# A kernel's opening rearranged: all of x ahead of the weights, and a first chunk of eight plain block products

## The chip, the cores and the metric

One core of one Trainium2 chip runs the whole program. The metric is the device time of one execution in microseconds (us). The kernel before takes 1982.69 us, the median of three runs (1981.05 to 1983.4). Every run is named fast, slow or unknown by its time and clock.

## The reference

```python
def reference(x, moe_w_in, moe_w_out):          # x (8, 3008, 256) f32; weights f64
    X = np.fft.fft(np.fft.fft(x, axis=1), axis=2).real.astype(np.float32)
    h = X.reshape(24064, 256) @ moe_w_in          # 256 x 2048
    g = h * np.clip(h + 3.0, 0.0, 6.0) / 6.0      # hardswish
    return (g @ moe_w_out).astype(np.float32)     # 2048 x 256
```

## The kernel before

The Fourier transform along the sequence (3008 = 47 x 64) is done in two stages of matrix products, for two batches (a pair) at a time; the one along the model dimension is folded into w_in. The MLP then goes over the tokens in chunks of eight steps. The steady state is full of TensorE work, and the change leaves it alone. What it touches is the opening.

Some filler products keep TensorE awake until the first data are there. Then eight blocks of x go through stage 1. Seven of them use `fold_first` and `stage1_first`; the last block (number 7) needs the longer `fold`. The products of stage 1 use 94 rows and 96 columns of the 128 x 128 array (`PR` = 94, `PZ` = 96).

```python
def stage1_first(pr, c, i):
    ...
    for k, (f, m, c0) in enumerate([(F[0:PR, 0:PZ], a[:, :, 0:P + 1], 0), (F[0:PR, 0:PZ], b, 1),
                                    (F[0:PR, 0:PZ], a[:, :, 1:P], P + 1), (FN[0:PR], b, P + 1)]):
        nc.tensor.matmul(ps[0:PZ, :, c0:c0 + m.shape[2]], f, m, start=(k == 0), stop=(k > 0),
                         skip_group_check=True)
    evict_z(pr, c, i, ps)      # ACT copies into a tile z; the queue SP writes it to DRAM
    ...
def keep_awake(n):
    ps = ps_h.tile([P, 2 * TB], F32, tag="uv", name="awake")
    for i in range(n):
        nc.tensor.matmul(ps[:], ones[:], Z[:], start=True, stop=True)
...
keep_awake(6)
```

The f64 weights come in 16 pieces, and each is converted by four engines: ACT takes the exponents out of the raw bits (`exponent_a`), TensorE joins them (`exponent_b`, called ex below), ACT shifts them back (`exponent_c`), VectorE takes the mantissa and multiplies (`mantissa`, `join`). Every second piece of w_in is followed by a fold of eight products of 0.43 us, whose last row travels through DRAM into the tile WN. Before the change, one piece lies behind each block of stage 1 and eight more follow:

```python
for c in range(NXC):
    if c + 2 < NXC:
        load_x(first, c + 2)
    load_w(c + 2)
    ...                               # fold_first, or fold for the last block
    on_scalar(c)                      # exponent_c of the piece before, exponent_a of this one
    on_vector(c)                      # mantissa, join
    for i in range(XC // 2):
        (stage1_first if c < NXC - 1 else stage1)(first, c, i)
    on_tensor(c)                      # exponent_b, and a fold after every second w_in piece
    ...
load_g(first, 0)                      # reads the results back for stage 2
for j in range(NXC, 15):              # seven more pieces (the sixteenth ahead of the first chunk)
    ...
```

A step of the MLP is `mlp1` (products u and v, made two steps ahead, then VectorE, two relus on ACT, two gates on VectorE), `combine` (sums on GpSimd) and `mlp2`: seven products in place of eight, in the manner of Strassen, for which w_out needs four combinations (`mix_w_out`, on VectorE).

## Time and profile before

| | before |
|---|---|
| median of 3 runs | 1982.69 us |
| span of the profiled run | 1978.3 us |
| TensorE busy | 1949.1 us, 99% of the span |
| first product of stage 1, last one | 10.5 us, 53.7 us |
| ninth set of seven products, the first behind the first chunk | 134.96 us |

The page names engines PE (TensorE matmul), PEld (its weight loads), DVE (VectorE), ACT (ScalarE), POOL (GpSimd) and SP (SyncE). L204 means line 204. In the chain of waits each line is a start, a duration, an engine and what it did; the chain is the work that ended last, followed backwards. In a timeline, the bracket at the end is how long the engine stood idle before, and what ended that. In the windows, PEclk is the granted TensorE clock as a share of full speed. The lines of before are shown in the prediction.

### The profile page before, as it was taken

Reading aid. Unit: us, or ns where it says so; the run is one execution under the profiler, and the core shown is the slowest. Engines: PE = TensorE matmul, PEld = TensorE weight load, DVE = VectorE, ACT = ScalarE, POOL = GpSimd, SP = SyncE. Lnnn points to the kernel's source line nnn. Section 1 sums busy time; section 2 is a strip of 40 time slices with the busy share of each in tenths; the row PEclk is TensorE's granted clock in tenths of the full one; section 3 lists DMA queues with packets and bytes.
Section 4 is the critical chain, followed back from the end, with each engine's and each line's share of the span. In section 5 each row is a group of like instructions: output and inputs, shape, how many; then the busy total and the mean of one; then the engine's idle time right before and its main releaser. Section 6 shows DMA issues by size and latency. Waiting matters only on the chain.

```text
span 1978.3 us, 27746 instructions
## 1 busy us (share of the span) xinstructions
PE 1949.1 (99%) x9178; PEld 1685.4 (85%) x9178; DVE 1433.5 (72%) x2775; ACT 687.9 (35%) x1164; POOL 1414.2 (71%) x1604
## 2 busy tenths in 40 slices
PE   8899999999999999999999999999999999999998
PEld 5588888888998888888898888888889888888887
DVE  5677767776787776776777776777678777777776
ACT  6533333333333333333333333333333333333332
POOL 4277778786687787777768877778667667666765
PEclk9999999999999999999999999999999999999999
DMA  9502211111111111221111221212110101111000
GB/s 307 136 26 61 51 41 46 49 49 35 27 36 51 41 49 48 54 59 24 36 32 30 63 55 44 56 41 54 37 22 23 30 14 25 26 24 28 17 20 20
DMA packets 149701, 93.31 MB, mean 47 GB/s; under 512 B 121739, under 2 KB 135055, under 8 KB 149558
## 3 DMA queue, kind: packets, MB, share of 16 engines
q1 hardware_dynamic: 139294, 57.86, 12.2%
q0 software_dynamic: 9472, 33.49, 5.9%
q8 instruction: 72, 1.18, 0.2%
q14 instruction: 71, 0.58, 0.1%
q10 hardware_dynamic: 792, 0.20, 0.0%
HBM read 54.19 MB, written 37.33 MB: 46 GB/s over the span
## 4 chain that ended last, share of the span: by engine, by line
PE 93%; DVE 2%; ACT 1%; issue 0%; DMA 0%; SPq 0%; DVEq 0%; ACTq 0%
PE acc L403 56%; PE v L334 16%; PE u L334 16%; PE ps L284 2%; PE ps L227 2%; DVE a L379 1%; DVE s L339 1%; ACT t L376 0%; ACT PM L509 0%; DVE o L461 0%; PE wps L574 0%; DVE u L360 0%; PE ps L224 0%; PE ex L514 0%; PE awake L597 0%
## 5 line engine op out<-in xcount | busy, mean ns | idle before, releaser
L393 POOL TENSOR_TENSOR c<-a 128x512 f32<-128x512 f32 (+1 forms) x383 | 478.2, 1248 | 431.4 <-PE acc L403 369.3
L403 PE MATMUL acc<-c,G 128*128 128x256 f32 (+1 forms) x3072 | 712.0, 375 | 0.0
L376 ACT ACTIVATE t<-u,half 128x512 f32<-128x512 f32 (+1 forms) x384 | 261.0, 680 | 1100.5 <-DVE u L349 1018.7
L403 PEld LDWEIGHTS acc<-c,G 128*128 128x128 f32 x3072 | 577.5, 190 | 72.7
L339 DVE SCALAR_TENSOR_TENSOR s<-qn,WN,u 128x256 f32<-128x256 f32 (+1 forms) x768 | 330.0, 471 | 354.3 <-PE u L334 354.0
L403 PE MATMUL acc<-a,G 128*128 128x256 f32 (+1 forms) x2304 | 551.2, 375 | 0.0
L403 PEld LDWEIGHTS acc<-a,G 128*128 128x128 f32 x2304 | 433.8, 190 | 55.9
L334 PE MATMUL v<-q,W 127*128 127x256 f32 (+1 forms) x1536 | 390.1, 376 | 4.4 <-DVE a L379 4.4
L334 PE MATMUL u<-q,W 128*128 128x256 f32 (+1 forms) x1536 | 388.3, 375 | 2.4 <-DVE a L379 2.1
L379 DVE SCALAR_TENSOR_TENSOR a<-t,u 128x512 f32<-128x512 f32 (+2 forms) x448 | 263.7, 600 | 104.9 <-ACT t L376 102.1
L334 PEld LDWEIGHTS u<-q,W 128*128 128x128 f32 x1536 | 285.7, 190 | 58.2 <-issue 14.8
L334 PEld LDWEIGHTS v<-q,W 127*128 127x128 f32 x1536 | 288.7, 190 | 45.1 <-DVE a L379 4.1
L393 POOL TENSOR_TENSOR c<-c,a 128x256 f32<-128x256 f32 (+1 forms) x383 | 274.8, 717 | 30.0
L393 POOL TENSOR_TENSOR c<-a,c 128x256 f32<-128x256 f32 (+1 forms) x383 | 274.6, 717 | 30.1
L349 DVE TENSOR_TENSOR u<-s,v 128x512 f32<-128x512 f32 x352 | 245.0, 696 | 37.7 <-PE v L334 0.8
L379 DVE SCALAR_TENSOR_TENSOR a<-t,v 128x512 f32<-128x512 f32 (+1 forms) x480 | 263.2, 564 | 0.0
L376 ACT ACTIVATE t<-v,half 128x512 f32<-128x512 f32 (+1 forms) x384 | 260.5, 678 | 0.0
L351 DVE TENSOR_TENSOR v<-v,s 128x512 f32<-128x512 f32 x352 | 243.7, 692 | 0.0
L393 POOL TENSOR_TENSOR r<-w,e 128x256 f32<-128x256 f32 (+1 forms) x94 | 90.8, 987 | 3.7
L411 ACT ACTIVATE e<-acc 128x512 f32<-128x512 f32 (+2 forms) x190 | 86.3, 545 | 3.4 <-PE acc L403 3.3
L461 DVE STREAM_TRANSPOSE o<-r 128x256 f32<-128x256 f32 (+1 forms) x192 | 72.5, 414 | 0.2
L239 ACT COPY z<-ps 96x512 f32<-96x512 f32 x64 | 37.2, 582 | 83.7 <-PE ps L227 65.2
(91 smaller groups left out, 780.2 us busy)
## 6 DMA issues: line engine op xcount, KB each, us to landing
out_dram<-o SPq DMA_DIRECT2D x746, 32.0 KB
zd<-z SPq DMA_DIRECT2D x32, 384.0 KB
g<-zd SPq DMA_DIRECT2D x48, 256.0 KB
xt<-in_x_dram POOLq DMA_DIRECT2D x21, 384.0 KB, 4.1
qn<-qd SPq DMA_DIRECT2D x19, 256.0 KB
st<-in_moe_w_in_dram POOLq DMA_DIRECT2D x8, 512.0 KB, 9.1
st<-in_moe_w_out_dram POOLq DMA_DIRECT2D x8, 512.0 KB, 5.1
xt<-in_x_dram POOLq DMA_DIRECT2D x7, 376.0 KB, 3.9
```

What stands on the lines that cost most here:

```text
L227: nc.tensor.matmul(ps[0:PZ], F[0:PR, 0:PZ], y[:, 2 * i:2 * i + 2, :], start=True, stop=True)
L284: nc.tensor.matmul(ps[:, blk, u * P:n].rearrange("p (b k) -> p b k", b=2), g[:, kk, blk * (P + 1):blk * (P + 1) + P], T[:, :, gr, blk, kk, ...
L334: nc.tensor.matmul(ps[:, i, 0:nq], W1[r, blk, f * P:(f + 1) * P], q[r, blk, of:of + nq], start=True, stop=True)
L339: nc.vector.scalar_tensor_tensor(s[:, i, 0:nq], qn[:, of:of + nq], WN[:, f:f + 1], u[:, i, 0:nq], op0=AL.mult, op1=AL.add)
L349: nc.vector.tensor_tensor(u[:], s[:], v[:], op=AL.add)
L351: nc.vector.tensor_tensor(v[:], v[:], s[:], op=AL.subtract)
L376: nc.scalar.activation(t, h, AF.Relu, bias=half[:], scale=scale)
L379: nc.vector.scalar_tensor_tensor(dst, t, 1.0, h, op0=AL.min, op1=AL.mult)
L393: (eng or nc.gpsimd).tensor_tensor(out, in0, in1, op=AL.add)
L403: nc.tensor.matmul(ch.acc[i // 2][:, i % 2, 0:ch.n], G[:, i, fc, :], mv, start=(fc == 0 and i % 2 == 0), stop=(fc == NF - 1), skip_group_c ...
L411: nc.scalar.mul(ch.e[:, k:i + 1, 0:ch.n], ch.acc[i // 2][:, 0:i + 1 - k, 0:ch.n], 1.0 / WS)
L461: nc.vector.transpose(o[:, 0:n // DH, h], ch.r[:, m, h, 0:n].rearrange("p (j i) -> p j i", i=DH))
```

## The change

The intent: load all of x first, so that stage 1 runs without weights between, with the longer block 7 at its front; put the conversion of the weights behind it, mostly into the steps of the first chunk; let that chunk use eight plain block products, which need no combinations; and make the combinations later, on GpSimd. Its core:

```diff
+    def mlp2_first(ch, fc):
+        a = ch.a.pop(fc)
+        for h in range(2):
+            ...
+            for f in range(2):
+                nc.tensor.matmul(ch.acc[h][:], G[:, (B11, B12, B21, B22)[2 * f + h], fc, :], a[:, :, f], ...)
...
     def exponent_b(j):
-        ex = ps_h.tile([P, WB], F32, tag="uv", name="ex")
+        ex = ps_h.tile([P, WB], F32, tag="uv", name="ex") if starting[0] else bank([P, WB], "ex")
...
     def mix_w_out(j):
-        tt = nc.vector.tensor_tensor
+        tt = nc.gpsimd.tensor_tensor
...
+    order = [NXC - 1] + list(range(NXC - 1))
+    for c in order[0:6]:
+        load_x(first, c)
+    load_forward(first, order[6])
+    for k, c in enumerate(order):
+        if k > 0:
             fold_first(first, c)
         else:
             for part in range(2):
                 fold(first, c, part, nc.vector)
-        on_scalar(c)
-        on_vector(c)
         for i in range(XC // 2):
-            (stage1_first if c < NXC - 1 else stage1)(first, c, i)
-        on_tensor(c)
+            (stage1_first if k > 0 else stage1)(first, c, i)
...                                  # seven weight loads between, behind x
     load_g(first, 0)
-    for j in range(NXC, 15):
...
+    for j in range(4):
+        convert(j)
...                                  # stage 2, spread, convert(4)
-    mlp1(*chunk(1))
...
+    convert(5)
+    convert(6)
...
+        if s < NF:
+            flush_copies()
+            mlp1(*chunk(s + 1))
+            convert(2 * s + 7)
+            mlp2_first(*chunk(s))
+            convert(2 * s + 8 if s < 4 else None)
+            if s >= 4:
+                mix_w_out(s - 4)
```

More of the change, by code (lines that the diff above doesn't have):

```diff
@@ L51 @@
 NK1 = (N1 + 1) // 2
+B11, B21, B12, B22 = 0, 1, 3, 6
 PROD = ("P1", "P2", "-P4", "P5", "P7", "-P6", "P3")
@@ L124, in __init__, with x_tile @@
             self.g, self.q, self.qn = {}, {}, {}
-    def x_tile(pr, i):
+    def x_tile(pr, c, i):
+        i += 2 * (c if pr.p > 0 else (c + 1) % NXC)
         pool, tag = xpool, "x"
@@ L140, in load_forward @@
     def load_forward(pr, c):
-        xt = x_tile(pr, 2 * c)
+        xt = x_tile(pr, c, 0)
         nr = PR + 2 if pr.p < NP - 1 else PR
@@ L151, in load_partners @@
     def load_partners(pr, c):
-        xr = x_tile(pr, 2 * c + 1)
+        xr = x_tile(pr, c, 1)
         pr.xr[c] = xr
@@ L231, in evict_z @@
         if i == 0:
-            pool, tag = (gpool, "g") if pr.p == 0 and c % 3 == 2 else (zpool, "z")
+            pool, tag = (gpool, "g") if pr.p == 0 and c % 3 == 1 else (zpool, "z")
             pr.z[c] = pool.tile([PZ, XC, D], F32, tag=tag, name="z")
-            if c == 0:
+            if pr.zd is None:
                 pr.zd = dpool.tile([2, NK1, 2, NS, D], F32, tag="zd", name="zd")
@@ L311, in __init__ @@
             self.last = ck == NCK - 1
+            self.first = ck == 0 and pr.p == 0
             self.final = self.last and pr.p == NP - 1
@@ L393, in add @@
         (eng or nc.gpsimd).tensor_tensor(out, in0, in1, op=AL.add)
+    def mlp2_first(ch, fc):
+        a = ch.a.pop(fc)
+        for h in range(2):
+            if fc == 0:
+                ch.acc[h] = ps_a.tile([P, 2, TB], F32, tag="acc", name="acc")
+            for f in range(2):
+                nc.tensor.matmul(ch.acc[h][:], G[:, (B11, B12, B21, B22)[2 * f + h], fc, :], a[:, :, f],
+                                 start=(fc == 0 and f == 0), stop=(fc == NF - 1 and f == 1))
+        if fc == NF - 1:
+            ch.r = epool.tile([P, 2, 2, TB], F32, tag="r", name="r")
+            for h in range(2):
+                for m in range(2):
+                    nc.scalar.mul(ch.r[:, m, h], ch.acc[h][:, m], (1 - 2 * m) / WS)
     def mlp2(ch, fc):
@@ L479 @@
     WB = 512
-    PIECES = [("in", 0), ("in", NWI // 2), ("out", 0), ("in", 1), ("in", NWI // 2 + 1)]
-    PIECES = [(k, n, i) for k, n in PIECES + [("out", j) for j in range(1, NWO)] for i in range(2)]
+    PIECES = [("in", 0), ("in", NWI // 2), ("out", 0), ("out", 1), ("in", 1), ("in", NWI // 2 + 1)]
+    PIECES = [(k, n, i) for k, n in PIECES + [("out", j) for j in range(2, NWO)] for i in range(2)]
     assert NWI == 4 and NWO == 4
@@ L486, in load_w @@
         kind, n, i = PIECES[j]
-        st = wpool.tile([P, 2 * WB], I32, tag="st", bufs=4, name="st")
+        pool, tag, bufs = (wpool, "st", 4) if j % 7 < 4 else (cpool, "c", None)
+        st = pool.tile([P, 2 * WB], I32, tag=tag, bufs=bufs, name="st")
         o = st[:].bitcast(moe_w_in.dtype)
@@ L537, in join @@
             return
-        b12 = wpool.tile([P, 2, P], F32, tag="b12", bufs=2, name="b12")[:] if i == 0 else None
-        for h, g in enumerate((block(n, 0), b12) if i == 0 else (block(n, 1), block(n, 6))):
+        for h, g in enumerate((B21, B22) if i else (B11, B12)):
             f, e = (t.rearrange("p (c q h e) -> h p c q e", c=2, h=2, e=DH)[h] for t in (frac, ex))
-            nc.vector.tensor_tensor(g.rearrange("p c (q e) -> p c q e", e=DH), f, e, op=AL.mult)
-        if i == 0:
-            w[PIECES[j]] = b12
+            nc.vector.tensor_tensor(block(n, g).rearrange("p c (q e) -> p c q e", e=DH), f, e, op=AL.mult)
     def block(j, i):
         return G[:, i, 2 * j:2 * j + 2, :]
-    def use_pair(j):
-        kind, n, _ = PIECES[2 * j]
-        if kind == "in":
-            fold_w_in(n)
-        else:
-            mix_w_out(n)
     def mix_w_out(j):
-        b12 = w.pop(("out", j, 0))
         g = [block(j, i) for i in range(7)]
-        tt = nc.vector.tensor_tensor
-        tt(g[3], g[0], b12, op=AL.subtract)
-        tt(g[5], g[6], g[3], op=AL.add)
-        tt(g[2], g[5], g[1], op=AL.subtract)
-        tt(g[4], g[6], b12, op=AL.subtract)
+        tt = nc.gpsimd.tensor_tensor
+        tt(g[4], g[B22], g[B12], op=AL.subtract)
+        tt(g[3], g[B11], g[B12], op=AL.subtract)
+        tt(g[5], g[B22], g[3], op=AL.add)
+        tt(g[2], g[5], g[B21], op=AL.subtract)
     def fold_w_in(n):
@@ L571, in fold_w_in @@
         for blk in range(2):
-            ps = bank([P, WB], "wps")
+            ps = bank([P, WB], "wps") if starting[0] else spare[blk]
             for i in range(2):
@@ L580, in copy @@
             nc.sync.dma_start(out=wn[n:n + 1], in_=W1[P - 1:P, 1, cs])
+            nb = WB // P
+            nc.sync.dma_start(out=WN[:, n * nb:(n + 1) * nb], in_=wn[n].rearrange("(j p) -> p j", p=P))
         copies.append(copy)
-    def load_wn(n):
-        nb = WB // P
-        nc.sync.dma_start(out=WN[:, n * nb:(n + 1) * nb], in_=wn[n].rearrange("(j p) -> p j", p=P))
     def load_t(gr):
@@ L622 @@
     wn = dpool.tile([NWI, WB], F32, tag="wn", bufs=1, name="wn")
-    load_forward(first, 0)
-    load_partners(first, 0)
-    load_w(0)
-    load_x(first, 1)
-    load_w(1)
     pending, copies = [], []
@@ L639, in on_scalar, with flush_copies @@
             exponent_a(j)
+        flush_copies()
+    def flush_copies():
         while copies:
@@ L652, in on_tensor, with convert @@
         done = pending.pop() if pending else 0
-        if done % 2:
-            use_pair(done // 2)
+        if done % 2 and PIECES[done][0] == "in":
+            fold_w_in(PIECES[done][1])
         if j is not None:
             pending.append(j)
-    for c in range(NXC):
-        if c + 2 < NXC:
-            load_x(first, c + 2)
-        load_w(c + 2)
-        if c < NXC - 1:
+    def convert(j):
+        if j is not None and j >= len(PIECES):
+            return
+        on_scalar(j)
+        on_vector(j)
+        if starting[0]:
+            keep_awake(1)
+        on_tensor(j)
+        if j is not None and j + 7 < len(PIECES):
+            load_w(j + 7)
+    order = [NXC - 1] + list(range(NXC - 1))
[4 more added lines that the diff above has]
+        if k > 0:
             fold_first(first, c)
@@ L666 @@
                 fold(first, c, part, nc.vector)
-        on_scalar(c)
-        on_vector(c)
         for i in range(XC // 2):
-            (stage1_first if c < NXC - 1 else stage1)(first, c, i)
-        on_tensor(c)
-        if c == 0:
-            load_t(0)
-        if c in (4, 6):
-            load_wn(PIECES[c - 4][1])
-    load_g(first, 0)
-    for j in range(NXC, 15):
-        if j < 14:
-            load_w(j + 2)
-        on_scalar(j)
-        on_vector(j)
-        keep_awake(1)
-        on_tensor(j)
-    load_wn(PIECES[6][1])
-    load_wn(PIECES[8][1])
-    load_g(first, 1)
-    load_t(1)
-    keep_awake(2)
+            (stage1_first if k > 0 else stage1)(first, c, i)
+        if k == 0:
+            load_partners(first, order[6])
+        elif k == 1:
+            load_x(first, order[7])
+            load_t(0)
+            for j in range(4):
+                load_w(j)
+        elif k in (4, 5):
+            for j in ((4, 5), (6,))[k - 4]:
+                load_w(j)
+    load_g(first, 0)
+    for j in range(4):
+        convert(j)
     for i in range(2):
@@ L691 @@
     spread(first, 0)
+    convert(4)
     starting[0] = False
+    spare = [ps_a.tile([P, WB], F32, tag="acc", name="spare") for blk in range(2)]
+    flush_copies()
     chunks = [[Chunk(pr, ck) for ck in range(NCK)] for pr in pairs]
     NST = 2 * NF
-    after = {}
     def beside(p):
@@ L706, in beside @@
         cur = pairs[p]
+        late = 4 if p == 0 else 0
         if p == 0:
-            for f in (on_scalar, on_vector, on_tensor):
-                after.setdefault(1, []).append((f, (None,)))
-            for gr in range(2, NG):
-                after.setdefault(gr, []).append((load_t, (gr,)))
+            put(2, load_g, cur, 1)
+            for gr in range(1, NG):
+                put(gr + 1, load_t, gr)
             put(NF - 1, close_w)
@@ L721, in beside @@
                 put(NST * (gr - 2) + 12, load_g, cur, gr)
-            s2(NST * (gr - 1), cur, gr)
+            s2(NST * (gr - 1) + (late if gr == 1 else 0), cur, gr)
         if p + 1 < NP:
@@ L725, in beside @@
             for c in range(NXC):
-                put(9 * c, load_x, nx, c)
-                put(9 * c + 3, fold, nx, c, 0, nc.gpsimd)
-                put(9 * c + 5, fold, nx, c, 1, nc.gpsimd)
+                t = 2 * late + (9 - late // 4) * c
+                put(t, load_x, nx, c)
+                put(t + 3, fold, nx, c, 0, nc.gpsimd)
+                put(t + 5, fold, nx, c, 1, nc.gpsimd)
                 for i in range(XC // 2):
-                    put(9 * c + 8 + 3 * i, stage1, nx, c, i)
+                    put(t + 8 + 3 * i, stage1, nx, c, i)
             put(NST * (NG - 1) - 2, load_g, nx, 0)
@@ L747, in chunk @@
         return chunks[p][ck], fc
-    on_scalar(15)
-    on_vector(15)
     mlp1(*chunk(0))
-    mlp1(*chunk(1))
-    on_tensor(15)
-    combine(*chunk(0))
+    convert(5)
+    convert(6)
     prev = None
@@ L760 @@
             f(*a)
-        if s + AHEAD < len(steps):
-            mlp1(*chunk(s + AHEAD))
-        if s + 1 < len(steps):
-            combine(*chunk(s + 1))
-        if prev and fc < 3:
-            finish(prev) if fc == 0 else store(prev, fc - 1)
-        mlp2(*chunk(s))
-        for f, a in after.get(s, ()):
-            f(*a)
+        if s < NF:
+            flush_copies()
+            mlp1(*chunk(s + 1))
[4 more added lines that the diff above has]
+                mix_w_out(s - 4)
+            if s == NF - 1:
+                mlp1(*chunk(NF + 1))
+                combine(*chunk(NF))
+        else:
+            if s + AHEAD < len(steps):
+                mlp1(*chunk(s + AHEAD))
+            if s + 1 < len(steps):
+                combine(*chunk(s + 1))
+            if prev and fc < 3:
+                if fc > 0:
+                    store(prev, fc - 1)
+                elif not prev.first:
+                    finish(prev)
+            mlp2(*chunk(s))
         if fc == NF - 1:
```

## The prediction

> **What bounds the kernel now.** I read the page's busy shares first, then the chain that ended last, the waits of the first 130 us, and the busy times in 2 us windows.
>
> ```profile
> span 1978.3 us, 27746 instructions
> ## 1 busy us (share of the span) xinstructions
> PE 1949.1 (99%) x9178; PEld 1685.4 (85%) x9178; DVE 1433.5 (72%) x2775; ACT 687.9 (35%) x1164; POOL 1414.2 (71%) x1604
> ```
>
> PE is the bound, so only what PE must do, and where it waits, can count. The chain in order of time shows the opening and the steady loop:
>
> ```profile
> 48.94 0.09 DVE y L174
> 49.03 0.14 issue
> 49.17 1.99 PE ps L227 x2
> ...
> 61.73 0.47 issue
> 62.20 1.41 ACT PM L509 x2
> 63.65 0.38 PE ex L514
> 64.03 3.43 PE wps L574 x8
> 67.46 0.86 PE awake L597 x2
> ...
> 133.23 0.86 PE u L334 x4
> 134.09 0.86 PE v L334 x4
> 134.96 3.02 PE acc L403 x14
> 137.98 0.86 PE u L334 x4
> ```
>
> From 109 us on, a step of the MLP is u 0.86, v 0.86 and seven accumulated products 3.02: 4.75 us back to back, with nothing else but small stage work of 0.86 to 0.91. PE is full there, and the change leaves those 376 steps alone. What can move is the opening, up to the end of the first chunk (132.37, where its eighth set of products ends). It has three parts: stage 1 of the first pair with eight weight pieces between (10.5 to 53.7), eight more pieces (to 76), then stage 2 and the first chunk. In the first, the vector engine's folds wait for x:
>
> ```profile
> DVE y L189 <- DMA xt<-in_x_dram,IX: 16.6, 7, 5.5
> ```
>
> In the windows, the columns are PE, PEld, DVE, ACT, POOL busy, then the PE clock, DMA share and GB/s:
>
> ```profile
> 30.00:32.00 2.00, 2.00 (x11) 1.39 (x10) 1.45 (x5) 1.44 (x4) 0.52 (x1) 1.00 1.08 353
> ...
> 50.00:52.00 2.00, 2.00 (x5) 1.04 (x4) 1.93 (x4) 0.58 (x1) 0.72 (x1) 0.50 0.53 143
> ...
> 86.00:88.00 2.00, 0.76 (x4) 0.14 (x2) 1.88 (x4) 0.58 (x1) 1.88 (x2) 1.00 0.00 0
> ...
> 90.00:92.00 2.00, 2.00 (x6) 1.55 (x6) 0.87 (x2) 0.00 (x0) 1.90 (x3) 0.50 0.85 209
> ```
>
> The DMA engines are full until 50 us, and after a stretch in which PE was little used its clock falls to half.
>
> **What the Trainium skill says.** "TensorE: Matmul & The Clock Gate", Part 1: after an idle window of about 3.4 us the array runs at half clock until a busy window has passed. The trace agrees, and a shorter gap is enough: PE stood for 2.87 us before 49.17 and the clock is 0.50 from 50 to 54; from 82 to 90 PE worked under half of the time and it is 0.50 from 90 to 92. "DMA: Bandwidth & Descriptors", Issuing engines are not separate DMA queues: all queues share 16 engines, so weights sent early delay x. Agrees: share 1.0 while x and weights alternate. "GPSIMD Engine Reference", 3.1: a two-input add takes about twice VectorE's time. Agrees: 128x256 takes 0.73 us on POOL, 0.42 on DVE when undisturbed.
>
> **The change part by part.**
>
> *Stage 1 without weights.* x is 16 loads of 0.385 MB = 6.2 MB. Before, the same time carries also the weights. Eight pieces' exponent products (0.43 each) and two folds of w_in (3.43 each) leave this part of PE. A c of stage 1 is 16 matmuls at 0.215 = 3.44 us of PE; DVE needs 1.4, ACT 1.5. The first fold starts when the first pair has landed, 9.1 as before; it is now the longer last block (2.5 us to the first matmul), so PE starts at 11.65, needs 2.15 for that block, then 7 x 3.44 = 24.1: 37.9. Transfers at the 330 GB/s seen from 10 to 50 us: after 9.1 about 4.8 MB of x, 2.7 MB of results and 0.3 of tables before the last block, 7.8 MB / 0.33 = 24 us, so it lands near 33 when it is wanted at 33. I add 1 us: stage 1 ends at **38.9** instead of 53.7. Gain 15 us.
>
> *Four pieces, stage 2, a fifth piece.* All 16 pieces now lie behind stage 1. The cycle of one piece is ACT exponent down 0.5, ACT exponent up 1.4, PE 0.43: 2.36 us from 69.28 to 71.64 in the trace. From the end of stage 1: copy and column 0.9; pieces 0 to 2 in 6.5, then fold 3.43, awake 0.86, piece 3 0.43: 12.2; stage 2 and spread 1.78 + 0.91: 14.9; ACT copy of qn, then down 0.5 and up 1.4 of pieces 3 and 4 and product 0.43: 17.85; second fold 3.43: 21.3; first u and v: 23.0. The last row of the second fold goes through DRAM to WN: ACT copy ends at 21.9, a write of 2 KB lands in 1.2 (qd, 128.26 to 129.43), the read I estimate at 2.4: 25.5. Only then can DVE make s: 0.87, u 0.6, relus 1.35: 28.5; then ACT pieces 4 to 6 before PE's next: 1.9 + 0.45 + 1.9 + 0.43: **33.1** after stage 1.
>
> *Steps 0 to 3, two pieces each.* PE's order is u v of the next step, product of piece 2s+7, eight block products, product of piece 2s+8. ACT's is relus, then the pieces. So PE's second item waits for the first: u v 1.73; from the end of v to the end of both relus 2.1 (92.06 to 94.17); then a single PSUM bank holds the exponents, freed when DVE has done gates 0.65, mantissa 1.1 and join 0.75: 2.5 (ACT's own 0.5 + 1.4 lies beside it). Then 0.43, eight products 16 x 0.216 = 3.46 (seven: 3.02), 0.43. Sum 10.65 where PE's own work is 6.05. Four steps: 42.6. Two folds of w_in: 6.9. The second feeds u v of step 4 at once: copy 0.5 and WN by DRAM again, 3.3. Sum **53.3**.
>
> *Steps 4 to 7 and after.* Step 4 has one piece: 10.2. Steps 5 to 7 have none, and their inputs were made a step before: 3 x 5.2 = 15.6. Two small parts, u v once more and half of the next stage 2: 2.6. The combinations of w_out on POOL, four times four adds of 0.75, lie beside this; the last set of three writes ends 2.4 after the chunk, its combine 1.3 later: 3.7, when PE wants it 4.8 later. Hidden. The first chunk needs no combinations and no finish, which were hidden anyway. So the eighth product costs 8 x 0.43 = 3.5, already in the 3.46 of each step.
>
> *Sum.* 38.9 + 33.1 + 53.3 + 10.2 + 15.6 + 2.6 = 153.7; half a stage 2 is still owed (0.9): 154.6, against 132.4. **22 us lost.**
>
> *The clock.* In steps 0 to 4 PE stands for 4.6 us at a stretch, and 7 us before step 0. By the two places above, the clock should fall in most of them and stay at half for 3 to 6 us of work, 1.5 to 3 us lost each time. Five gaps give up to 11; some may escape, and I take 8. So 1982.7 + 22 + 8 = **2013**.
>
> **Rivals.** (1) The intended outcome: pieces fit into gaps, and the first chunk is PE bound. Then steps 0 to 3 cost 4 x 6.05 + 6.9 = 31 instead of 53, step 4 5.6, no cold clock, and the sum is about 128: 4 us faster than before, 1979. For it: ACT works 35% and DVE has room (6.8 us of work in a step of 10.65). Against it: ACT takes its queue in order, and the exponents stand behind relus that wait for PE and DVE. (2) The transfers stay the bound: stage 1 no longer interleaves weights, but results and weights 0 to 3 share the engines; at 290 GB/s the last block lands 3 to 4 us late, 2016. (3) POOL becomes the bound in the first pair, whose folds come every 8 steps instead of 9: per 8 steps combinations 22.8, finish 4.75, folds 5.3, issues 1.8: 34.7 of 38 us. It fits, so nothing. (4) The PE clock stays full: 2005.
>
> **Range and chances.** From 1997 (no cold clock and one third of the serial waits absent) to 2025 (transfers late, every gap cold and longer). A gain of 2% is 40 us, and rival 1, the best case that I can construct, wins 4, so faster by over 2% gets 0.01. Slower by 2% begins at 2022.3, 9 us above my figure: 0.18.
>
> **What would show it.** Stage 1's last matmul near 39 us. First block product near 38.9 + 33.1 + 1.73 + 2.1 + 2.5 + 0.43 = 78.8 or some us later. In the first chunk, waits of PE's exponent product for ACT or DVE, about 4.6 us a step, and of DVE's s for the DMA of WN, twice, about 3 us. PE clock of 0.5 several times between 60 and 130. Each step after the ninth again 4.75. End of the first chunk's products near 155 to 165. It would be wrong if the pieces ran ahead of the relus on ACT, if WN's round trip were much shorter or longer, if x landed well after 33, or if the steady loop changed at all.

## The result, and the profile after

The changed kernel takes 2043.62 us (median of four runs, 2042.06 to 2045.18) and the kernel before, on the same chip, 1981.87 us (1980.93 to 1983.4). The ratio is 1.0311, with a 95% interval from 1.0293 to 1.0329: slower by 3.1%. A ratio here and below is the mean time of one kernel's fast runs over that of the other's of the same rounds, so it is not quite the ratio of the medians that are quoted. The prediction was 2013 us, in a range of 1997 to 2025, and not slower by over 2%: the kernel lost about 62 us where 30 were expected.

The page of the changed kernel: the span, the busy time of PE, and the PE clock in 40 slices (tenths).

```profile
span 2041.0 us, 27582 instructions
PE 1982.3 (97%) x9122; PEld 1691.9 (83%) x9122; DVE 1427.1 (70%) x2759; ACT 688.6 (34%) x1164; POOL 1399.6 (69%) x1591
...
PEclk6778999999999999999999999999999999999999
```

PE is busy for 33 us longer, with 56 matmuls fewer. That is what a slow clock looks like: much the same work takes longer and counts as busy. The clock digits of the first four slices (204 us) are 6 to 8; before, all 40 were 9 (0.90 or more). The chain of waits in order of time shows where:

```profile
16.13 47.61 PE ps L204 x112
...
85.44 1.12 DMA wn<-W
86.57 2.09 DMA WN<-wn
...
104.35 1.04 PE ex L537 x2
105.39 5.50 PE acc L408 x8
...
174.50 3.44 PE acc L408 x8
```

The seven shorter blocks of stage 1 (112 matmuls, L204) run back to back for 47.61 us, 0.425 us each, where the prediction had 0.215 each. The block products of a step (L408) take 5.50 us in one step, the first 4.0 of them at half clock, and 3.44 in another, at full clock. The windows of 5 us show it directly (columns PE, PEld, DVE, ACT, POOL busy, then the PE clock, DMA share, GB/s):

```profile
60.00:65.00 5.00, 5.00 (x11) 2.79 (x10) 0.00 (x0) 1.79 (x4) 0.00 (x0) 0.50 0.00 1
65.00:70.00 5.00, 3.53 (x9) 1.13 (x8) 2.41 (x4) 4.07 (x8) 1.27 (x2) 1.00 0.73 217
```

PE is busy for 5.00 of 5.00 us and its clock is 0.50. In finer windows it is so from 13.85 to 65.05 us, and 1.00 from there to 88.9. The last products in this stretch are not stage 1's: behind stage 1, from 63.74 us on, come filler products of 128 rows and 128 columns, and the clock rises 1.3 us into them. The timeline of PE shows what came before the fall, and one of the waits in the steps:

```profile
12.67 1.10 PE L231 MATMUL ps<-y,F 94*96 94x512 f32 x2 [2.97 <-DVE y L178]
...
117.72 1.03 PE L537 MATMUL ex<-PM,E 128*128 128x512 f16 x2 [4.67 <-DVE wi L558]
```

PE stood for 2.97 us between the filler and the first product of stage 1. In the kernel before this gap was 0.54 us in the profiled run (the filler ended at 9.99, the first product began at 10.53):

```profile
10.53 0.68 PE L200 MATMUL ps<-xt,F 94*96 94x258 f32 x2 [0.54 <-DVE xt L191]
```

Of the 2.43 us more, 1.05 are the longer fold, since the change puts the block that needs it first (2.47 us from the start of the fold to the first product, 1.42 before); 1.09 are x, whose first fold started at 10.20 us and not at 9.11; and 0.3 are the filler, which ended at 9.70. The second line of the changed kernel is the wait of the exponent product: 4.67 us.

Against the terms of the prediction:

| Stretch | predicted us | measured us | difference |
|---|---|---|---|
| up to the end of stage 1 | 38.9 | 63.7 | +24.8 |
| from there to step 0 | 33.1 | 33.0 | 0 |
| steps 0 to 4, with the cold (half) clock | 53.3 + 10.2 + 8 = 71.5 | 63.5 + 12.55 = 76.0 | +4.5 |
| steps 5 to 7 | 15.6 | 15.5 | 0 |
| two small parts: u, v once more, and half of stage 2 | 2.6 | 2.6 | 0 |
| v of step 8 waits for DVE | not named | 1.5 | +1.5 |

The sum of the differences is 30.8 us, and the miss was 2043.62 - 2013 = 30.6 (they agree more closely than the parts deserve: the kernel before ran 0.8 us faster beside this run than in the three runs that the prediction started from). In the traces, the set of products behind the first chunk begins 59.5 us later (194.42 against 134.96), and the small parts that the opening still owes at that point are half of stage 2 (0.89) and a part of stage 1 (0.86). That is 61.2 of the 62.7 us between the two spans; where the last 1.5 us lie I have not traced. The steady loop is unchanged: PE is busy for 1703.94 us in the last 1718 us before, and for 1704.21 in the last 1719 after.

### The profile page after: what moved, and what is told of

Same layout as the page of the kernel before. It is cut to its first block, busy times and chain, and to the rows that moved or that the text cites. A ratio compares the mean times of both kernels' runs of the same rounds, so it can differ in the third digit from the quotient of the medians.

```text
span 2041.0 us, 27582 instructions
## 1 busy us (share of the span) xinstructions
PE 1982.3 (97%) x9122; PEld 1691.9 (83%) x9122; DVE 1427.1 (70%) x2759; ACT 688.6 (34%) x1164; POOL 1399.6 (69%) x1591
## 4 chain that ended last, share of the span: by engine, by line
PE 94%; DVE 3%; ACT 1%; DMA 1%; issue 1%; SPq 0%; DVEq 0%; ACTq 0%
PE acc L424 53%; PE u L339 15%; PE v L339 15%; PE ps L204 2%; PE ps L288 2%; PE ps L231 2%; PE acc L408 2%; DVE a L384 1%; DVE s L344 1%; ACT t L381 1%; PE ex L537 0%; DVE o L482 0%; PE spare L587 0%; PE wps L587 0%; DMA xt<-in_x_dram,IX 0%
## 5 line engine op out<-in xcount | busy, mean ns | idle before, releaser
L398 POOL TENSOR_TENSOR c<-a 128x512 f32<-128x512 f32 (+1 forms) x375 | 467.9, 1248 | 398.8 <-PE acc L424 362.4
L424 PE MATMUL acc<-c,G 128*128 128x256 f32 (+1 forms) x3008 | 696.9, 374 | 0.0
L424 PEld LDWEIGHTS acc<-c,G 128*128 128x128 f32 x3008 | 565.4, 190 | 71.1
L424 PE MATMUL acc<-a,G 128*128 128x256 f32 (+1 forms) x2256 | 539.0, 375 | 0.0
L424 PEld LDWEIGHTS acc<-a,G 128*128 128x128 f32 x2256 | 424.1, 190 | 54.4
L398 POOL TENSOR_TENSOR c<-c,a 128x256 f32<-128x256 f32 (+1 forms) x375 | 268.9, 717 | 29.4
L398 POOL TENSOR_TENSOR c<-a,c 128x256 f32<-128x256 f32 (+1 forms) x375 | 268.7, 717 | 29.4
```

What stands on the lines that cost most here:

```text
L398: (eng or nc.gpsimd).tensor_tensor(out, in0, in1, op=AL.add)
L424: nc.tensor.matmul(ch.acc[i // 2][:, i % 2, 0:ch.n], G[:, i, fc, :], mv, start=(fc == 0 and i % 2 == 0), stop=(fc == NF - 1), skip_group_c ...
```

## The experiments

All edits are on the changed kernel unless the kernel before is named. Every kernel gave the right result. "Clock" is the mean granted clock over the whole run. In the traces the clock changes only at edges that lie 3.413 us, or a multiple of it, apart (the 51.2 us at half clock are fifteen times that); such a stretch is called a window below.

**Is it the gap ahead of stage 1?** My theory: the gap of 2.97 us drops the clock, and the 94 x 96 products cannot raise it again. Three more filler products shorten the gap.

```diff
-    keep_awake(6)
+    keep_awake(9)
```

> The changed kernel with 9 instead of 6 of the unused warm-up products at the start, so that PE works until about 12.3 us and the gap before the first stage-1 product shrinks from 2.97 us to about 0.4. Theory (the gap dropped the clock, and stage 1's 94x96 products hold a full clock but cannot raise a half one): clock 1.0 through stage 1, its last product ends near 39 us instead of 63.7, 24 to 25 us gained: about 2018 us. Rival (products of 94x96 are too light to hold the clock when nothing else is between them): the clock falls a window later, stage 1 ends near 60, about 2039 us.

Measured: 2026.93 us (2023.89 to 2030.33, four runs; before 1980.31), ratio 1.024 (1.022 to 1.0259). By the spans, 18.9 us are won. The first product of stage 1, then the chain of this kernel, then ACT's longest wait in it:

```profile
12.74 1.10 PE L231 MATMUL ps<-y,F 94*96 94x512 f32 x2 [1.41 <-DVE y L178]
```

```profile
15.14 3.45 PE ps L204 x16
...
19.23 9.56 DMA zd<-z
...
29.96 12.60 DMA zd<-z
...
50.65 6.28 DMA g<-zq
```

```profile
39.78 1.07 ACT L243 COPY z<-ps 96x512 f32<-96x512 f32 x2 [6.49 <-DMA zd<-z]
```

The gap is 1.41 us (the 0.4 expected did not come about, for the filler itself ended at 11.33), and that is short enough: 16 products take 3.45 us, the clock is 1.00 to the end of stage 1, and its last product ends at 39.06 us, the 38.9 of the prediction. So the gap is the cause of the slow stage 1. But stage 2 begins only at 56.96 us: the chain has left PE for the transfers. Two writes of z take 9.56 and 12.60 us to land, ACT waits three times for a z tile to come free (2.46, 6.49 and 1.46 us), and the read of g lands at 56.9. The slow stage 1 had hidden this. From the end of stage 1 to step 0 it is now 39.6 us (39.06 to 78.61), where the slow kernel had 33.0.

**Does a burst of wide products in mid-stage raise the clock?**

```diff
+        if k == 2:
+            keep_awake(4)
```

> The changed kernel with four unused 128x128 products of 512 columns after the third block of stage 1 (near 29.7 us), inside the stretch at half clock. Theory (94x96 products cannot raise the clock, full ones can): the clock comes back within one or two windows of 3.4 us after the burst starts and stays; the five blocks left take 3.44 us each instead of 6.8: the burst costs about 5 and the blocks save 17, stage 1 ends near 52, about 2031 us. Rival (the clock is held down by something else, such as the full DMA engines or a stuck state): it stays at 0.5, the burst adds 6.8, about 2049 us.

```profile
30.09 4.90 PE awake L608 x8
34.99 17.22 PE ps L204 x80
```

Yes. Four products of 128 x 128 (each shows as two matmuls) raise it: the eight take 4.90 us, where the rate of the slow burst in the next experiment but one, 10.45 us for twelve, would make 7.0. The 80 stage-1 matmuls behind them take 0.215 each. Stage 1 ends at 52.2 us and the kernel takes 2033.45 us (two runs; ratio 1.0267). So a full clock, once there, is held by the same 94 x 96 products that could not raise it in 49.9 us of the changed kernel (13.85 to 63.74).

**Is it the columns?** I thought of the area in use, 94 x 96 of 128 x 128, and widened the stage-1 weights to 128 columns (the further columns hold other table values, and their outputs are not read).

```diff
-        for k, (f, m, c0) in enumerate([(F[0:PR, 0:PZ], a[:, :, 0:P + 1], 0), ...
+        for k, (f, m, c0) in enumerate([(F[0:PR, 0:P], a[:, :, 0:P + 1], 0), ...
```

> The changed kernel with stage 1's weights 128 columns wide instead of 96 (the 32 more rows of PSUM are never read; results stay right); the same instructions and the same gap before them. Theory (the share of the array in use decides whether a half clock is raised, and 94x96 is too little): the clock falls at 13.9 as before and comes back within two windows, by about 21 us; stage 1 ends near 43, about 2022 us. Rival (columns do not count: rows, or gaps between products, or something outside PE): no change, 63.7 and about 2042 us.

```profile
17.02 47.62 PE ps L204 x112
```

Measured: 2044.7 us (two runs; ratio 1.0324), and the 112 matmuls stay at half clock. More columns alone do not raise it.

**Rows or columns, in one run.** Three bursts of six products of 512 columns of data: 94 rows x 128 columns behind the second block, 128 x 96 behind the fourth, 128 x 128 behind the sixth.

```diff
+        if k in (1, 3, 5):
+            rows, cols = {1: (PR, P), 3: (P, PZ), 5: (P, P)}[k]
+            pa = ps_h.tile([P, 2 * TB], F32, tag="uv", name="burst%d" % k)
+            for _ in range(6):
+                nc.tensor.matmul(pa[0:cols], ones[0:rows, 0:cols], Z[0:rows], start=True, stop=True)
```

> The changed kernel with three bursts of six unused products of 512 columns inside stage 1: after the second block of 94 rows x 128 columns of the array, after the fourth of 128 rows x 96 columns, after the sixth of 128x128 (zeros and ones, as the warm-up; 10.2 us each at half clock, so each holds two whole windows of 3.4 us). e2_burst showed that 128x128 raises the clock, e3_cols that more columns alone do not. Theory (rows in use decide): 0.5 through the first burst, 1.0 within the second and after. Rival (the whole area decides): 0.5 through both, 1.0 in the third. Rival (the shape does not count, but short products of 254 columns with a weight load each): 1.0 within the first burst. By time about 2050 for the first, 2060 for the second, 2040 for the third.

```profile
22.70 10.45 PE L693 MATMUL burst<-Z,ones 94*128 94x512 f32 x12
...
46.54 5.64 PE L693 MATMUL burst<-Z,ones 128*96 128x512 f32 x12
52.02 0.60 PE L204 MATMUL ps<-xt,F 94*96 94x258 f32 x2
```

Twelve matmuls with 94 rows take 10.45 us, all at half clock, though they fill two whole windows and most of a third. With 128 rows and only 96 columns the clock is at 1.00 from 47.2 us, 0.65 us into the burst, and the stage-1 products behind are at full speed. So rows raise it and columns do not, unless it is the area after all: 128 x 96 uses 12288 cells of the array and 94 x 128 nearly as many, 12032. Against the area speaks that the window which ended in the rise held 2.76 us of 94 x 96 products and 0.65 of the burst, by time a mean of some 9600 cells, fewer than the windows full of 94 x 128 that ended without a rise. This counts only if a window is judged by its mean, which is not shown. (One run, 2048.81 us: it carries the bursts.)

**How many rows?** Bursts of 98, 106 and 117 rows at the same places. In the first try (2033.11 us, one run) the gap ahead of stage 1 happened to be 1.79 us, the clock did not fall, and all three bursts took some 5.3 us at full clock: nothing was tested, except that the opening of the changed kernel escapes the fall where its gap is shorter.

> The changed kernel with three bursts of six 512-column products onto 128 columns in its half-clock first stage: 98 rows after the second block, 106 after the fourth, 117 after the sixth. The run with bursts of 94 x 128, 128 x 96 and 128 x 128 left two readings: a share of the 128 rows just above 94 (such as three quarters, 96) is the limit, or all or nearly all rows are needed. Theory A (limit between 94 and 98): the first burst, at about 22.7 us, ends at full clock after 6 to 8 us instead of 10.45, and the stage ends near 50. Theory B (limit above 98): the first burst takes 10.4 us at half clock and a later one raises it: the 106 burst if it takes under 9 us at about 46.6, else the 117 burst. Theory C (only all 128): all three take 10.4 us and the stage ends near 95, the kernel at about 2070.

The second try has two filler products fewer at the start, so that the gap is long (it was 5.07 us).

```diff
-    keep_awake(6)
+    keep_awake(4)
...
-            rows, cols = {1: (PR, P), 3: (P, PZ), 5: (P, P)}[k]
+            rows, cols = {1: (98, P), 3: (106, P), 5: (117, P)}[k]
```

> The run before this (bursts of 98, 106 and 117 rows) tested nothing: by chance its gap ahead of the first stage was 1.79 us and the clock stayed at 1.0 throughout. This kernel has two filler products fewer at the start, so that the gap is some 4 us or more and the clock falls. Theory A (limit between 94 and 98 rows): the first burst, 98 rows, starts at half clock and takes 6 to 8 us instead of 10.4; the first stage ends near 53. Theory B (limit higher): the first takes 10.4 us and the 106 or the 117 burst is the first under 9 us. Theory C (only all 128): all three take 10.4 us, the kernel near 2070. If the first stage starts at full clock again, the run is void.

```profile
23.23 6.44 PE L693 MATMUL burst<-Z,ones 98*128 98x512 f32 x12
29.51 0.60 PE L204 MATMUL ps<-xt,F 94*96 94x258 f32 x2
```

The clock was 0.50 from 11.87 us, and 98 rows raised it, to 1.00 at 25.49 us, 2.3 us into the burst. (One run, 2040.77 us.) So 94 rows do not raise the clock and 98 do. The rise lies on the grid of 3.413 us: 13.62 us, four windows, after the fall, as that of the run before came ten windows (34.1 us) after its fall, 13.08 to 47.19. Both windows that ended in a rise began with 94-row products. If the mean over a window counts, which is my reading and not shown, this one had (1.15 x 94 + 2.26 x 98) / 3.41 = 96.7 rows, and the limit lies between 94 and 96.7. A limit of area between 12032 and 12288 cells would fit all these bursts as well (98 x 128 is 12544), if one product above it in a window were enough. Three quarters of the rows, 96, would fit; no run was made at that number. The bursts multiply zeros by ones, so these values at least do raise a clock.

**Does the longer first block make the gap?** The blocks in their natural order, with block 7 last as before.

```diff
-    order = [NXC - 1] + list(range(NXC - 1))
+    order = list(range(NXC))
```

(With the tiles reassigned to match.) 

> The changed kernel with the long last block of x folded last again, as before the change, and all else as changed. Its short first fold lets PE start near 11.6 instead of 12.7 us. Theory (gap): a gap of 1.9 us does not drop the clock, stage 1 ends near 39 to 40, about 2018 us. Rival (it is the missing exponent products and weight folds between the blocks that let the clock fall): the clock falls all the same, about 2042 us.

Two runs gave 2025.63 and 2041.66 us, sixteen apart. I repeated it in five rounds, to see whether these are two groups.

> e4_last once more, five rounds. Its two runs gave 2025.6 and 2041.7 us at mean clocks of 0.986 and 0.975, as e1_fill and as the changed kernel. Theory (its gap of 1.5 us before the first product of stage 1 falls now inside one window of the clock's monitor, now across two, and only the first drops the clock, for all of stage 1): two groups of times, near 2025 at 0.986 and near 2042 at 0.975, nothing between. Rival (one slow outlier): all near 2026.

The six runs were 2043.65, 2043.83, 2029.6, 2043.8, 2025.98 and 2041.86 us, with clocks of 0.974, 0.974, 0.986, 0.974, 0.986 and 0.975. The ratio of 1.0274 mixes two groups, and I don't use it. The profiled runs fell in different groups. The first products of stage 1 in the first, then in the second:

```profile
11.26 0.68 PE L204 MATMUL ps<-xt,F 94*96 94x258 f32 x2 [1.48 <-DVE xt L195]
```

```profile
11.44 0.68 PE L204 MATMUL ps<-xt,F 94*96 94x258 f32 x2 [2.58 <-DVE xt L195]
...
12.59 1.05 PE L204 MATMUL ps<-xt,F 94*96 94x254 f32 x2
```

A gap of 1.48 us kept the clock; one of 2.58 us lost it within 1.2 us of work, and the products then took 1.05 us per pair. So the two groups are real, but not for the reason I had, one gap of 1.5 us that falls now in one window and now across two. The fold began at almost the same time (9.84 and 9.97 us). What differs is the end of the filler, 9.78 and 8.86: the same twelve matmuls start every 0.85 us at first and every 0.43 later, and the change comes at about 7.2 us in the first run and 5.3 in the second. Over all the profiled runs the first fold also starts at anything from 9.11 to 10.64 us. With the long block first the gap is longer by its fold, and all four runs of the changed kernel fell, by their clocks of 0.974 to 0.976. Whether the length of the gap decides, or how much of it lies in one window, is not separated: where the clock stayed it was at most 1.1 us in one window, where it fell at least 1.8.

**The waits of the exponent products in the steps.** To the filler of the first experiment I add two edits: ACT takes the exponents of the step's first piece ahead of the relus of the step's `mlp1`, and the products of odd pieces get their own bank.

```diff
-        ex = ps_h.tile(...) if starting[0] else bank([P, WB], "ex")
+        ex = ps_h.tile(...) if starting[0] or j % 2 else bank([P, WB], "ex")
...
+            if j < len(PIECES):
+                on_scalar(j)
             mlp1(*chunk(s + 1))
-            convert(2 * s + 7)
+            if j < len(PIECES):
+                on_vector(j)
+                on_tensor(j)
```

> e1_fill with one order changed in steps 0 to 4 of the first chunk: ACT gets the first piece of a step ahead of the step's relus, and its exponent product goes to another PSUM bank, so that neither relus nor joins hold it up. Theory (the loss is ACT's and PE's queue order, u v -> relus -> exponent -> PE): PE's wait of 4.6 us a step falls to about 1, the clock stays up, a step takes about 7 us instead of 12 to 13 with the slow clock: some 22 us less than e1_fill, about 2005 us. Rival (ACT's or DVE's amount of work bounds the step): DVE's 6.9 us a step; not over 10 us gained, about 2018 us.

```profile
85.86 0.60 PE L537 MATMUL ex<-PM,E 128*128 128x512 f16 x2 [0.51 <-DVE G L564]
...
93.49 0.60 PE L537 MATMUL ex<-PM,E 128*128 128x512 f16 x2 [1.22 <-DVE wi L558]
```

The waits fall from 4.6 us to 0.51 and 1.22 here (a last one of 3.35 us, at 119.18, stays), and with them most of the cold clock goes too: steps 0 to 4 take 49.2 us in place of 75.2. The kernel takes 1997.37 us (before 1980.91), ratio 1.0089 (1.0072 to 1.0105), 8 us better than I had expected. So the serial waits that the prediction named were real, and cost some 26 us in that kernel, about 16 as waits and 10 as clock. The last two figures are an estimate, from the experiment that follows.

**The clock in the steps alone.** On top of the first experiment's filler, more of it in the gaps; the waits are left as they are:

```diff
+    keep_awake(6)                # ahead of step 0
...
             convert(2 * s + 7)
+            if s < 5:
+                keep_awake(4)
```

> e1_fill with four unused full products (3.4 us) in the 4.6 us gap of steps 0 to 4 and six before step 0; the waits themselves stay. Theory (each gap drops the clock for two windows of 3.4 us, which costs about 2.5 us of PE's work each, six times): clock 1.0 from 60 us on, 13 to 15 us less than e1_fill, about 2013 us. Rival (the time at half clock lies beside waits and costs nothing): no gain, 2027 us.

Measured: 2019.59 us (before 1980.91), ratio 1.0203 (1.0185 to 1.0221). Steps 0 to 4 take 65.3 us instead of 75.2: 10 us for the clock (one window at half clock is left in them). But the filler ahead of step 0 ran at half clock itself, took 7.69 us and delayed step 0 by 4.9 us (from 78.61 to 83.52), which I had not foreseen. Filler must be in the gap before the clock falls, and short.

**The transfers behind stage 1.** With the first experiment's filler, seven result tiles in place of four, and only four weight pieces in flight.

```diff
-            pool, tag = (gpool, "g") if pr.p == 0 and c % 3 == 1 else (zpool, "z")
+            pool, tag = zpool, "z"
+            if pr.p == 0:
+                pool, tag = ((gpool, "g"), (zpool, "z"), (qpool, "q"))[(0, 0, 1, 1, 2, 2, 2, 1)[(c + 1) % NXC]]
...
-        if j is not None and j + 7 < len(PIECES):
-            load_w(j + 7)
+        if j is not None and j + 4 < len(PIECES):
+            load_w(j + 4)
```

> e1_fill with seven instead of four buffers for stage 1's results and only four weight pieces in flight (piece j+4 is asked for when piece j has been used) instead of seven. Theory (with the clock up, the results' writes and the reads of stage 2's input wait in line behind 3.6 MB of weights: 5.4 us for the last write, 6.3 us for the read, ACT held 6.5 us by full buffers): no wait of ACT for writes of results, stage 2 starts near 50 instead of 57 us, 6 us gained, about 2021 us. Rival (the engines are full either way and the pieces then come late): no gain or a loss.

```profile
14.06 24.09 PE ps L204 x112
...
45.20 6.95 DMA g<-zq
```

The 112 products take 24.09 us, the 24.1 of the prediction, and ACT no longer waits for a z tile. Stage 2 begins at 52.28 us instead of 56.96. The kernel takes 2022.14 us, ratio 1.0211 (1.0194 to 1.0228): 4.8 us from the transfers, where 6 were expected.

**All remedies together.** The filler, the tiles, ACT's order, and the first piece ahead of the last block:

```diff
+        if k == NXC - 1:
+            on_scalar(0)
+            on_vector(0)
...
+    split(6, start_first)
...
-            mlp1(*chunk(s + 1))
-            convert(2 * s + 7)
+            split(2 * s + 7, lambda: mlp1(*chunk(s + 1)))
```

(`split` puts ACT's part of a piece ahead of `mlp1`, and the other parts behind it. Two more filler products follow the first `mlp1`.)

> All remedies together: the longer warm-up (e1_fill), ACT's pieces ahead of the relus and two PSUM banks for the exponents (e6_ahead), seven result buffers and four pieces in flight (e9_xfer), piece 0 begun before the last block of stage 1, and pieces 4 to 6 ahead of the first relus, so that they lie beside the DRAM round trip of WN. Theory (the parts add up): e6_ahead's 1997 less 5 for the transfers, less about 5 for the pieces begun early, less 6 to 8 for pieces 4 to 6 beside WN: 1978 to 1982 us, even with the kernel before (1981) or just under it. If the steps' clock also stays up, 1975. Rival (the gains are on the same wait, which then ends with the later of the two): 1990 us.

```profile
24.70 14.19 DMA zq<-zc
...
55.01 4.06 PE ps L290 x16
```

Measured: 1993.76 us (five runs; before 1983.15), ratio 1.0055 (1.0039 to 1.007). That misses the 1978 to 1982 that I had expected, and is no gain over the kernel before. The small writes of one column (1.5 KB in runs of 4 bytes) now hold ACT: one took 14.19 us to land behind x, and ACT stood for 2.15 us at its end. The read of g still lands only at 55.0 us, PE stands idle before it, and stage 2 then takes 4.06 us where 1.80 to 2.1 were seen elsewhere, since the clock fell again. By this chain, the single gains were not additive because they ended on the same wait for the transfers; no run takes that wait away altogether.

**Would the filler help the kernel before?** It has a stretch at half clock at 50 us. Three fillers ahead of its last block:

```diff
+        if c == NXC - 1:
+            keep_awake(3)
```

> The kernel before with three unused full products (2.6 us) in its own gap of 2.87 us before the last block of stage 1, where its clock fell for 6.8 us. Theory (what was learned of the clock holds there too): clock 1.0 from 46 to 56 us, the last block of stage 1 ends 2 us earlier and the pieces after it start so: 1979 against 1981 us, at the edge of what five rounds show. Rival (the pieces behind it are bound by ACT and their weights): no difference.

Measured: 1981.38 us (before 1982.26), ratio 0.9993 (0.998 to 1.0006): the same. The clock stays full from 40 to 88 us, but the pieces behind stage 1 are bound by ACT, so TensorE only waits longer. No version that I ran beats the kernel before.

The opening of this run shows more. By chance its gap ahead of stage 1 was 2.05 us, and the clock fell in the kernel before as well, at 12.91 us:

```profile
11.28 0.68 PE L200 MATMUL ps<-xt,F 94*96 94x258 f32 x2 [2.05 <-DVE xt L191]
...
16.63 1.06 PE L514 MATMUL ex<-PM,E 128*128 128x512 f16 x2
```

But here a piece of the weights lies behind every block. The first window at half clock held 94-row products alone and ended without a rise; the second held the 128-row product of the piece, and at its end, 19.73 us, the clock was full again. So the kernel before pays two windows for such a gap, where the changed kernel paid fifteen: what the change took out of stage 1 is also what had raised the clock there.

## Why the prediction was wrong, point by point

- **The bound and the direction: right.** The steady loop did not move, the change lost time in the opening, and the intended outcome (rival 1) did not come about: the exponent products wait 4.62, 4.67, 4.67, 7.36 and 4.73 us in the steps where "about 4.6 us a step" stood. Steps 5 to 7 and the stretch from stage 1 to step 0 are right to 0.1 us. Within the latter two errors nearly cancel: the round trip through DRAM was 0.4 us shorter than the text had it (write 1.12 and read 2.09 us, against 1.2 and 2.4), and from there to the end of the relus it was 0.4 longer (3.4 against 3.0).
- **Stage 1: the step that failed.** "PE starts at 11.65, needs 2.15 for that block, then 7 x 3.44 = 24.1: 37.9" takes the full clock for granted. Measured: 47.61 us for the seven blocks, and the end at 63.7. The same text had seen the clock fall after PE stood for 2.87 us, but did not ask what the gap ahead of stage 1 would be. By its own numbers it was 1.66 us (the filler of before ends at 9.99), and gaps of 1.48 and 1.79 us kept the clock; measured, the first product came at 12.67 and the gap was 2.97. The fold took the 2.5 us of the text; it was x that came late, the first fold starting at 10.20 and not "9.1 as before", a figure read from one run. So one microsecond in the start of the first block decided 24.8 of the 30.6 us, and the text gave that possibility no weight. With the gap closed, the stage ends at 39.06 us: the arithmetic of the work was right.
- **How long it stays: also failed.** "stay at half for 3 to 6 us of work" was read from places where 128-row products follow. The clock stayed at half for 51.2 us, fifteen windows of 3.41 us; fourteen of them held only 94-row products, which did not raise it, and in the last came the filler of 128 rows. Nothing in the profile of before showed this plainly: there, 128-row products of the weights lay between the blocks. That part could not be read off the trace; that there was a gap could.
- **The clock in steps 0 to 4: right in kind, mis-sized.** "Five gaps give up to 11; some may escape, and I take 8." None of the five escaped, and the clock was at half from 88.9 to 99.2 us as well. Each fall lasted two windows (6.8 us: 102.6 to 109.4, 116.2 to 123.05, 133.3 to 140.1, 150.3 to 157.1, 164.1 to 170.9), and the term was 12.5, if the whole excess of these steps is put down to the clock; the filler in the gaps won 10 of it in its own kernel.
- **Rival 2, the transfers: half right.** x landed as predicted (the last fold stops waiting at 33.55 us in the kernel with the filler), but the writes of z and the read of g cost 4.8 us (what seven tiles won) to 5.9 us (24.8 less the 18.9 that the filler won) once stage 1 was quick. The slow stage 1 hid them. Rival 3 stayed nothing, as predicted: an addition of the combinations takes 0.73 us on GpSimd, and nothing waits for it.
- **Rival 4 and the range.** The rival "the PE clock stays full: 2005" was put to the steps only. The upper end, 2025, held "every gap cold and longer", but not a cold stage 1, and a loss of over 2% was given a chance of 0.18.

What stays open: 1.5 us of the difference between the spans; whether rows or area decide, and the exact limit (between 94 and 98 rows, if rows); whether the length of a gap counts or its share of one window; and why the first x tile lands earlier in some runs.

## What to carry to other kernels

When a change moves a longer first job ahead of the first product, move the end of the filler with it: three filler products were worth 17 us here. A gap of 2 to 3 us ahead of a long stretch of 94-row products cost not two windows but the whole stretch, since such a product held a full clock but did not raise a half one; a few products with all rows in its midst repair it. The length of such a gap varied by over a microsecond between runs of one kernel, so one profile does not tell whether it is safe. And remove the waits one by one and together: gains that end on the same later wait, here the transfers, do not add.

## What the Trainium skill lacked or had wrong

- "TensorE: Matmul & The Clock Gate", Part 1, says that the clock is full again after one busy window of about 3.4 us. It lacks the rows: products with 94 of 128 rows (and 96 columns) kept PE 100% busy for 49.9 us, fourteen whole windows and part of another, and the clock stayed at 0.50; 94 x 128 products did not raise it in 10.45 us; 98 x 128 and 128 x 96 did at the end of the window in which they began, 2.3 and 0.65 us in. (Rows, or an area of about three quarters: these runs do not fully separate them.) It lacks as well that 94-row products hold a full clock (24.09 us at 1.00).
- The same page, "Why this matters for your kernels", allows gaps up to about 3 us between bursts. Here 2.97, 2.58 and 2.05 us dropped the clock and 1.41, 1.48 and 1.79 us did not. Its free-running window (Part 1) agrees with the trace (edges at 13.85 and 65.05 us are fifteen windows of 3.413 us apart). One kernel fell in two groups, 2025.98 to 2029.6 and 2041.86 to 2043.83 us; the page's remark (Part 1) that the cost of the ramp is under 1% of a typical span is at its edge here: half clock cost stage 1 24.7 us (63.74 against 39.06), 1.2% of the span of before, and the kernel 18.9, 1.0%.
- "DMA: Bandwidth & Descriptors", Latency and other measured facts, gives 2 us at high load for the memory's latency. How long a small write waits in queues shared with large ones is far longer, and I found no figure for it there: a column write of 1.5 KB took 14.19 us to land while x was loading, and a result write of 384 KB 9.56 to 12.60, in the kernel with the longer filler, against 2.94 for the last one in the run with the burst, where stage 1 ended later.
